# Top-32 attention and a PReLU block on one core: other MLP blocks, the last two pairs interleaved, other ticks for the preparation steps, two casts on another engine

## The chip, the cores and the metric

The kernel runs on one core of a Trainium2 chip. The metric is device microseconds (us) of that core. The kernel before took 1068.87, 1069.68 and 1070.53 us in three runs; the median is 1069.68 us. Five engines work side by side, each through its own list of instructions in order: TensorE (PE; its weight loads are PEld), VectorE (DVE), ScalarE (ACT), GpSimd (POOL) and SyncE (SP), which here only issues DMAs.

## The reference

Eight batches, eight heads, 576 rows of 64. Each row of scores keeps what reaches its 32nd largest value; the rest is masked. The result goes, as 4608 tokens of 512, through two matrix products with a PReLU between them.

```python
scores = scale * np.matmul(q, k.transpose(0, 1, 3, 2))
kth = np.partition(scores, -top_k, axis=-1)[..., -top_k:-top_k + 1]
scores = np.where(scores >= kth, scores, -1000000000.0)
attn = np.exp(scores - np.max(scores, axis=-1, keepdims=True))
attn = attn / (np.sum(attn, axis=-1, keepdims=True) + 1e-09)
x = np.matmul(attn, v)                      # (8, 8, 576, 64) -> (4608, 512)
h = x @ w_in
g = np.maximum(h, 0.0) + alpha * np.minimum(h, 0.0)
out = g @ w_out
```

## The kernel before

Two heads make a pair; 32 pairs of 9 tiles (128 rows by 576 columns; the ninth holds the last 64 rows of both heads) make 288 tiles. One loop turn, a tick n, emits for every engine a little work on different tiles, and each engine runs what it was given in the order of emission. So the order of the work is written out by hand:

- PE: the scores of tile n+1 (`scores`, L290 and L295, into one of two PSUM buffers), then what the calendar has for PE in this tick, then one step of the queue `back`.
- ACT: what the step of `back` in the tick before left for it, then three passes over the scores of tile n: Sign with a running sum (`act_a`, tile h, L303), the calendar's ACT steps, Exp (`act_e`, tile e, L313), and the scores plus a bias (`act_b`, tile b, L319), which needs the bias `be`.
- POOL: the bias `be` from the sum of h (L306), y = b*h of tile n-1 (`pool_y`, L328), then the calendar's POOL steps.
- DVE: the 8 largest of each of six segments of y of tile n-2 (L336), a merge of tile n-3 to the 24 largest (L351, L353), every third tick a choice of the threshold KP (`select`, L360 to L369), the masked weights w of tile n-6 (`weights`, L381, which reads b, KP and e), then the calendar's DVE steps, and last a tiny write into the next y buffer (`mark`, L323), after which POOL may fill that buffer.
- SP: loads of q, k and v (`load`, L132 to L140), DMA transposes of w (L386 to L391) and of the attention output (`x_turn`, L468 and L470), and the stores of the output (L563).

The calendar (`put` and `run`) holds the preparation of the coming pairs. `prep_plan` gives each step a tick by the table `ts`, counted from the pair's first tile: transposes of q and k (`pe_q`, `pe_k`, `pe_t` with their copies on ACT), casts of k and v to bf16 on POOL (`pool_k`, tile kb, L160; `pool_v`, tile v_bf, L163), a cast of q on POOL (`pool_q`, tile qTb, L198), statistics of the scores (`pe_g` to `dve_1`), the start threshold T0 (`pool_1`, `pool_1b` with a power of 9 values, L243, `pool_1c` with L247 and L248, and `dve_2`, L251), and two biases from it (`pool_2`).

The product of weights and v (`av`) and its normalisation on DVE (`av_out`) come 5 to 7 ticks after the fourth and the ninth tile of a pair. When the fourth pair of a batch is done, `x_turn` turns the batch's output, and the MLP blocks (`blocks`: seven of 512 tokens, then 448, 320, 256) whose tokens are there are put into `back`: 16 steps of four matmuls (`ph_step`) and three steps for each 128 tokens (`pz_step`). After tile 287 the loop goes on until `back` is empty. At the end a sum over all checks becomes a flag that every engine loads (L678 to L686); it decides whether a general path runs.

Of the kernel before, what the change touches and what calls it, by code (L numbers as in the profile page):

```python
# [27 lines left out]
def kernel(  # L28
# [24 lines left out]
    NX = 2560  # L53
# [41 lines left out]
    v_bfs = [prep.tile([128, 10, V1], BF16, name=f"v_bf{i}", bufs=1) for i in range(3)]  # L95
# [30 lines left out]
    def load(p):  # L126
# [15 lines left out]
        pairs[p] = dict(q=st_q, k=st_k, st_v=st_v, v=v_bfs[p % 3])  # L142

    def prep_plan(p):
# [137 lines left out]
    def scores(n):  # L282
        p, j = divmod(n, TPP)
# [25 lines left out]
    def act_e(n):  # L309
        p, j = divmod(n, TPP)  # L310
# [30 lines left out]
    def merge_ops(n):  # L341
        p, j = divmod(n, TPP)
# [28 lines left out]
    def weights(n):  # L371
        p, j = divmod(n, TPP)
# [23 lines left out]
    def check_pair(p, put_late):  # L396
# [6 lines left out]
        nc.vector.scalar_tensor_tensor(out=DD[:, kt, :, 0], in0=KP[:, ns], scalar=-1.0,  # L403
                                       in1=KP[:, ns], op0=ALU.mult, op1=ALU.max)
# [4 lines left out]
    def check_batch(b):  # L409
# [6 lines left out]
        for i, (jk, src, lim, op) in enumerate((  # L416
# [5 lines left out]
                                    accum_out=good[:, b, i:i + 1])  # L422

# [40 lines left out]
    def x_turn(b):  # L464
        for i in range(5):
# [66 lines left out]
    def mlp_steps(t0, tb):  # L532
        c0 = t0 % NX
        hold = {}

        def ph_step(f):
            if f == 0:
                hold["gT"] = mlp.tile([128, NFT, 512], BF16, name="gT", tag="gT", bufs=1)
            hold[f] = ph = mlp_bank("ph", tb)
            for kk in range(NKT):  # L540
                nc.tensor.matmul(ph, w_in_b[:, kk, f * 128:(f + 1) * 128], xT[:, kk, c0:c0 + tb],  # L541
                                 start=(kk == 0), stop=(kk == NKT - 1))

        def ph_act(f):
            nc.scalar.activation(hold["gT"][:, f, 0:tb], hold.pop(f), AF.Relu)  # L545
# [19 lines left out]
        for f in range(NFT):  # L565
# [7 lines left out]
    blocks = [(512 * i, 512) for i in range(7)] + [(3584, 448), (4032, 320), (4352, 256)]  # L573
# [5 lines left out]
    with tc.manual_schedule(engines={E.PE, E.Activation, E.DVE, E.Pool, E.SP}):  # L579
# [241 lines left out]
```

## Time and profile before

| | |
|---|---|
| median of three runs | 1069.68 us |
| profiled execution, its time | 1068.65 us |
| its span, first to last instruction | 1066.9 us |
| DVE busy | 926.2 us, 87% |
| PE busy | 840.2 us, 79% |
| ACT busy | 805.6 us, 76% |
| POOL busy | 711.9 us, 67% |
| mean granted TensorE clock | 0.918 |

Busy shares are means over a start, a long even stretch and an end in which DVE has nothing to do. Which engine bounds a stretch is seen from the one that has no idle time in it, and from who waits for whom there.

### The profile page before, as it was taken

The page shows a single profiled execution, that of the slowest core. Times are in us where ns is not written, and L with a number is a line of the kernel's source. Part 1 is how long each engine was busy: PE and PEld are TensorE (multiplying, and loading weights), DVE is VectorE, ACT ScalarE, POOL GpSimd, SP SyncE. Part 2 cuts the span into 40 slices and gives each one's busy share as a digit, 9 for nine tenths or more (in the row PEclk, how much of TensorE's full clock was granted, in tenths as well). Part 3 has the DMA queues.
Part 4 walks back from the last instruction along what each step waited for, and adds up shares of the span by engine and source line. Part 5 has one row for each costly group of instructions (what it writes and reads, how often), then busy time and mean ns, then how long its engine had stood idle before and what let it go on. Part 6 is the DMA issues. An engine that isn't in the chain of part 4 may idle for free.

```text
span 1066.9 us, 20165 instructions
## 1 busy us (share of the span) xinstructions
PE 840.2 (79%) x5188; PEld 486.5 (46%) x5255; DVE 926.2 (87%) x5228; ACT 805.6 (76%) x1611; POOL 711.9 (67%) x988
## 2 busy tenths in 40 slices
PE   4667787778877897788877896778877896778995
PEld 3344444445444454444544553445444554444453
DVE  3699979999999999999999999999999999999000
ACT  3998867788778878788778877888778877884332
POOL 3787757778767776787777776787777776773000
PEclk9867897899979998999889998999889997999998
DMA  5697433535464445544444455535453455224200
GB/s 130 123 174 149 100 76 79 110 75 83 105 104 82 87 109 104 96 84 90 108 88 86 85 114 101 98 80 106 97 95 74 93 104 110 51 56 102 68 27 28
DMA packets 343021, 99.48 MB, mean 93 GB/s; under 512 B 335201, under 2 KB 335217, under 8 KB 342897
## 3 DMA queue, kind: packets, MB, share of 16 engines
q1 hardware_dynamic: 341744, 96.01, 44.8%
q0 software_dynamic: 1152, 2.10, 1.3%
q8 instruction: 44, 0.72, 0.3%
q14 instruction: 81, 0.66, 0.2%
HBM read 36.71 MB, written 9.44 MB: 43 GB/s over the span
## 4 chain that ended last, share of the span: by engine, by line
DVE 65%; POOL 13%; PE 11%; issue 5%; ACT 4%; DMA 1%; SPq 0%; POOLq 0%; ACTq 0%
DVE C L336 16%; DVE w L381 14%; DVE L L351 8%; DVE C L353 7%; POOL y L328 5%; POOL sq L243 5%; PE pz L557 3%; PE ph L541 3%; DVE pr L365 3%; DVE kk L368 3%; PE ps L290 3%; DVE wm L381 2%; DVE P L210 2%; DVE EQ L360 2%; DVE T L251 2%
## 5 line engine op out<-in xcount | busy, mean ns | idle before, releaser
L328 POOL TENSOR_TENSOR y<-b,h 128x576 f32<-128x576 f32 x288 | 368.0, 1278 | 142.3 <-DVE y L323 135.5
L290 PE MATMUL ps<-qkT 128*128 128x288 f32 x1024 | 349.3, 469 | 126.9 <-ACT b L319 125.9
L336 DVE MAX8 C<-y 128x8 f32<-128x96 f32 x1728 | 423.4, 245 | 16.2 <-POOL y L328 16.2
L290 PEld LDWEIGHTS ps<-qkT 128*128 128x128 f32 x1024 | 199.0, 211 | 243.7 <-ACT b L319 201.0
L319 ACT ACTIVATE b<-ps,be 128x576 f32<-128x576 f32 x288 | 213.8, 742 | 120.3 <-POOL be L306 117.9
L381 DVE SCALAR_TENSOR_TENSOR w<-b,KP,e 128x576 bf16<-128x576 f32 x256 | 225.0, 879 | 0.0
L313 ACT ACTIVATE e<-ps,nbe 128x576 bf16<-128x576 f32 x288 | 215.4, 748 | 7.7 <-POOL nbe L258 3.0
L303 ACT ACTIVATE h<-ps,T 128x576 bf16<-128x576 f32 x288 | 213.5, 741 | 6.9 <-DVE T L251 6.1
L306 POOL TENSOR_SCALAR be<-S_all,n2t 128x1 f32<-128x1 f32 x288 | 144.8, 503 | 94.5 <-ACT h L303 93.2
L351 DVE MAX8 L<-C 128x8 f32<-128x48 f32 x864 | 164.4, 190 | 0.1
L541 PE MATMUL ph<-xT,w_in_b 128*128 128x512 bf16 (+3 forms) x606 | 150.9, 370 | 3.4 <-issue 1.5
L557 PE MATMUL pz<-w_out_b,gT 128*128 128x512 bf16 (+1 forms) x564 | 137.9, 379 | 2.2 <-issue 1.1
L545 ACT ACTIVATE gT<-ph 128x512 bf16<-128x512 f32 (+3 forms) x160 | 88.7, 555 | 30.6 <-PE ph L541 29.1
L353 DVE MATCH_REPLACE8 C<-L,C 128x48 f32<-128x48 f32 x576 | 109.7, 190 | 0.0
L541 PEld LDWEIGHTS <-w_in_b 128*128 128x128 bf16 x640 | 58.4, 100 | 53.5 <-issue 10.9
L557 PEld LDWEIGHTS <-gT 128*128 128x128 bf16 (+1 forms) x592 | 54.9, 98 | 60.5
L562 ACT COPY o_sb<-pz 128x512 f32<-128x512 f32 (+1 forms) x37 | 21.6, 582 | 65.0 <-PE pz L557 65.0
L303 ACT ACTIVATION_READ_ACCUMULATOR h<-ps,T 128x1 f32 x288 | 59.9, 208 | 0.0
L243 POOL TENSOR_TENSOR sq<-sq,half 128x9 f32<-128x9 f32 x32 | 58.5, 1829 | 0.2
L684 DVE TENSOR_SCALAR bad<-ptot 1x1 int32<-1x1 f32 x1 | 0.1, 145 | 65.8 <-PE ptot L683 65.8
L436 PEld LDWEIGHTS <-wT 128*128 128x128 bf16 x1280 | 51.6, 100 | 11.3 <-DMA wT<-w 3.1
L436 PE MATMUL pu<-v_bf,wT 128*128 128x65 bf16 x1280 | 53.7, 197 | 2.8 <-DMA wT<-w 2.8
(106 smaller groups left out, 981.1 us busy)
## 6 DMA issues: line engine op xcount, KB each, us to landing
out_dram<-o_sb SPq DMA_DIRECT2D x35, 256.0 KB, 2.3
st_q<-in_q_dram SPq DMA_DIRECT2D x64, 128.0 KB, 2.8
kst<-in_k_dram SPq DMA_DIRECT2D x64, 128.0 KB, 2.6
st_v<-in_v_dram SPq DMA_DIRECT2D x64, 128.0 KB, 2.5
w_stage<-in_moe_w_out_dram SPq DMA_DIRECT2D x16, 256.0 KB, 3.9
w_in_b<-in_moe_w_in_dram POOLq DMA_DIRECT2D x8, 256.0 KB, 6.0
wT<-w SPq DMA_TRANSPOSE x128, 3.3
st_q<-in_q_dram SPq DMA_DIRECT2D x32, 32.0 KB, 2.5
```

The lines of the kernel that those rows point to most:

```text
L290: nc.tensor.matmul(ps[:, hf, 0:HC], T[:, 0, c0:c0 + 128], T[:, 1 + j % 2, ks], start=True, stop=True)
L303: nc.scalar.activation(halves(t["h"]), t["ps"], AF.Sign, bias=T0[:, n:n + 1], scale=-ONE_EPS, accum_out=S_all[:, n:n + 1])
L306: nc.gpsimd.tensor_scalar(t["be"], S_all[:, n:n + 1], 512.5, d["n2t"][:, j:j + 1], ALU.is_le, ALU.mult)
L313: nc.scalar.activation(halves(t["e"]), t["ps"], AF.Exp, bias=d["nbe"][:, j:j + 1], scale=scl)
L319: nc.scalar.activation(halves(t["b"]), t["ps"], AF.Identity, bias=t["be"])
L328: nc.gpsimd.tensor_tensor(t["y"], t["b"], t["h"], ALU.mult)
L336: return [lambda g=g: nc.vector.max(out=C[:, j, g, :], in_=t["y"][:, g * SEG:(g + 1) * SEG]) for g in range(NSEG)]
L351: ops.append(lambda r=r, src=src: nc.vector.max(out=L[:, 8 * r:8 * r + 8], in_=src))
L353: ops.append(lambda r=r, src=src: nc.vector.match_replace(out=C2, in_to_replace=L[:, 8 * r:8 * r + 8], in_values=src, imm_value=NEG))
L381: nc.vector.scalar_tensor_tensor(out=dst, in0=t["b"], scalar=KP[:, n:n + 1], in1=t["e"], op0=ALU.is_ge, op1=ALU.mult)
L541: nc.tensor.matmul(ph, w_in_b[:, kk, f * 128:(f + 1) * 128], xT[:, kk, c0:c0 + tb], start=(kk == 0), stop=(kk == NKT - 1))
L557: nc.tensor.matmul(pz[0:m], hold["gT"][:, f, r0:r0 + m], w_out_b[:, f, :], start=False, stop=(f == NFT - 1))
```

## The change

- The MLP blocks follow the batches: for every two batches 512, 512 and 128 tokens, and for the last two 512, 320 and 320. A block of 128 tokens does four columns of w_in in a step. The ring buffer xT has 2304 columns (four batches) instead of 2560.
- The tiles of the last two pairs alternate (`ORDER`), so that the first four tiles of both come first. Their first half of the output is turned by its own, and the first block of 320 waits for that half only. Pair 31 is loaded and prepared some ten ticks earlier.
- In a tick the step of `back` is emitted before the calendar's PE steps, and two steps a tick after the last tile.
- The table `ts` is another; `av` comes one tick later (three ticks after the weights at the very end).
- The casts of k and v are `nc.scalar.copy` on ACT (`act_kb`, `act_v`), between h and e of a tick; v_bf has four buffers, y three, C three.
- The flag at the end is computed and loaded inside the loop (`final_flag`), some ticks before the last block ends.

```diff
-    NX = 2560
+    NX = 2304
...
+    ORDER = [divmod(n, TPP) for n in range(NT - 2 * TPP)]
+    ORDER += [(NPAIR - 2 + s, 2 * i + h) for i in range(4) for s in range(2) for h in range(2)]
+    ORDER += [(NPAIR - 2, 8), (NPAIR - 1, 8)]
...
-        def pool_k():
+        def act_kb():
             d["kb"] = prep.tile([128, 5, 130], BF16, name="kb", tag="kbP", bufs=1)
-            nc.gpsimd.tensor_copy(d["kb"], d["k"])
-
-        def pool_v():
-            nc.gpsimd.tensor_copy(d["v"][:, :, 0:D], d["st_v"])
+            nc.scalar.copy(d["kb"], d["k"])
+
+        def act_v():
+            nc.scalar.copy(d["v"][:, :, 0:D], d["st_v"])
...
-            ts = [-14, -13, -12, -11, -10, -9, -6, -5, -4, -3, -2, -2, -1, -5]
+            ts = [-14, -13, -12, -11, -10, -9, -7, -6, -5, -4, -3, -2, -1, -8,
+                  -13 if p == 3 else -15]
...
     def scores(n):
-        p, j = divmod(n, TPP)
+        p, j = ORDER[n]
...
-        y = attn.tile([128, S], FP32, name="y", bufs=4)
+        y = attn.tile([128, S], FP32, name="y", bufs=3)
...
+    def final_flag():
+        tot = const.tile([128, 1], FP32, name="tot")
+        junkg = const.tile([128, B * 4], FP32, name="junkg")
+        nc.vector.tensor_scalar(junkg, good.rearrange("p a b -> p (a b)"), 1.0, None, ALU.mult,
+                                ALU.add, accum_out=tot)
+        bad = const.tile([1, 1], I32, name="bad")
+        pt = ps_d.tile([1, 1], FP32, name="ptot", tag="pd")
+        nc.tensor.matmul(pt, tot, ones_f, start=True, stop=True)
+        nc.vector.tensor_scalar(bad, pt, float(128 * NT * (3 + NSEG)) - 0.5, None, ALU.is_lt)
+        flag.append(nc.values_load(bad[0:1, 0:1], min_val=0, max_val=1))
...
-    blocks = [(512 * i, 512) for i in range(7)] + [(3584, 448), (4032, 320), (4352, 256)]
+    blocks = []
+    for i in range(0, NTOK, 2 * S):
+        blocks += [(i, 512), (i + 512, 512), (i + 1024, 128)]
+    blocks[-2:] = [(NTOK - 640, 320), (NTOK - 320, 320)]
...
-            run(n, "pe")
-            if back:
-                pe_f, after = back.popleft()
-                pe_f()
+            for _ in range(2 if n >= NT else 1):
+                if back:
+                    if after:
+                        after()
+                    pe_f, after = back.popleft()
+                    pe_f()
+            run(n, "pe")
...
+                        dt = 3 if n >= NT - 7 else dt
                         put(n + dt, "pe", lambda wp=wp, g=g: av(wp, g))
                         put(n + dt + 1, "dve", lambda wp=wp, g=g: av_out(wp, g))
+                        if last and (g == 1 or wp == NPAIR - 1):
+                            part = (range(5) if wp < NPAIR - 1 else (range(2), range(2, 5))[g])
+                            put(n + dt + 1, "dve", lambda b=b, part=part: x_turn(b, part))
+                            lim = (b + 1) * S if g == 1 else NTOK - 320
...
+                            put(n + dt + (4 if wp < NPAIR - 1 else 2), "end", feed)
```

What the table moves is seen in the order of instructions on POOL, in four ticks in the middle of the program. Before, with v_bf and kb the casts, sq the statistics and DD a check; each `be` begins a tick:

```order
L163 CAST v_bf_110<-st_v_107 128x10x64
L306 TENSOR_SCALAR be<-S_all,n2t 128x1
L328 TENSOR_TENSOR y<-b,h 128x576
L238 TENSOR_TENSOR sq<-MM 128x9
L239 TENSOR_TENSOR sq<-MM,sq 128x9
L240 TENSOR_SCALAR sq<-sq 128x9
L160 CAST kb<-kst_104 128x650
L306 TENSOR_SCALAR be<-S_all,n2t 128x1
L328 TENSOR_TENSOR y<-b,h 128x576
L243 TENSOR_TENSOR sq<-sq,half 128x9
L405 TENSOR_TENSOR DD<-DD,C 128x9x6
```

and from the third tick on:

```order
L243 TENSOR_TENSOR sq<-sq,half 128x9
L405 TENSOR_TENSOR DD<-DD,C 128x9x6
L306 TENSOR_SCALAR be<-S_all,n2t 128x1
L328 TENSOR_TENSOR y<-b,h 128x576
L247 TENSOR_SCALAR sq<-sq 128x9
L248 TENSOR_TENSOR t_7962<-sq,MM 128x9
L198 CAST qTb<-qkT_111 128x576
```

After the change the same stretch of POOL reads:

```order
L242 TENSOR_TENSOR sq<-MM 128x9
L243 TENSOR_TENSOR sq<-MM,sq 128x9
L244 TENSOR_SCALAR sq<-sq 128x9
L312 TENSOR_SCALAR be<-S_all,n2t 128x1
L334 TENSOR_TENSOR y<-b,h 128x576
L247 TENSOR_TENSOR sq<-sq,half 128x9
L312 TENSOR_SCALAR be<-S_all,n2t 128x1
L334 TENSOR_TENSOR y<-b,h 128x576
L251 TENSOR_SCALAR sq<-sq 128x9
L252 TENSOR_TENSOR t_8003<-sq,MM 128x9
L418 TENSOR_TENSOR DD<-DD,C 128x9x6
```

The casts v_bf and kb are gone from POOL; the power (L243 before, L247 after) and the two steps behind it stand one tick earlier against the pair, and qTb alone is left behind y in the fourth tick.

The two casts stand on ACT, in the second and the fourth tick of a pair; there before, and now:

```order
L303 ACTIVATE h,S_all<-ps,T_100 128x576
L313 ACTIVATE e<-ps,nbe 128x576
L319 ACTIVATE b<-ps,be 128x576
L562 COPY o_sb<-pz 128x512
L303 ACTIVATE h,S_all<-ps,T_100 128x576
L313 ACTIVATE e<-ps,nbe 128x576
```

```order
L309 ACTIVATE h,S_all<-ps,T_100 128x576
L167 CAST v_bf_109<-st_v_107 128x10x64
L319 ACTIVATE e<-ps,nbe 128x576
L325 ACTIVATE b<-ps,be 128x576
L309 ACTIVATE h,S_all<-ps,T_100 128x576
L319 ACTIVATE e<-ps,nbe 128x576
L325 ACTIVATE b<-ps,be 128x576
L593 COPY o_sb<-pz 128x512
L309 ACTIVATE h,S_all<-ps,T_100 128x576
L164 CAST kb<-kst_104 128x650
L319 ACTIVATE e<-ps,nbe 128x576
L325 ACTIVATE b<-ps,be 128x576
```

A cast stands behind h, whose sum POOL's `be` needs, and ahead of e and b.

At the end of the program SP's queue shows where the last batch's output is turned (xT, from xb and xm) among the transposes of w and the stores of the MLP's output (o_sb). Before, and now:

```order
L563 DMA out_dram<-o_sb 128x512
L391 DMA_TRANSPOSE wT<-w_15294 128x9x128
L386 DMA_TRANSPOSE wTm<-wm 128x5x128
L387 DMA_TRANSPOSE wTm<-wm 128x4x128
L563 DMA out_dram<-o_sb 128x512
L468 DMA_TRANSPOSE xT<-xb 128x4x128 x4
L470 DMA_TRANSPOSE xT<-xm 128x4x64
L563 DMA out_dram<-o_sb 128x512 x3
```

```order
L494 DMA_TRANSPOSE xT<-xb 128x4x128 x2
L594 DMA out_dram<-o_sb 128x512 x2
L397 DMA_TRANSPOSE wT<-w_15518 128x9x128
L594 DMA out_dram<-o_sb 128x512
L397 DMA_TRANSPOSE wT<-w_15578 128x9x128
L594 DMA out_dram<-o_sb 128x512
L392 DMA_TRANSPOSE wTm<-wm 128x5x128
L393 DMA_TRANSPOSE wTm<-wm 128x4x128
L392 DMA_TRANSPOSE wTm<-wm 128x5x128
L393 DMA_TRANSPOSE wTm<-wm 128x4x128
L494 DMA_TRANSPOSE xT<-xb 128x4x128 x2
L496 DMA_TRANSPOSE xT<-xm 128x4x64
```

Two of the five transposes now stand ahead of the last transposes of w, and the transposes of the last ninth tiles stand behind the stores of the block that runs at that time.

## Rows read from the trace of the kernel before

**Rows 1.** The page's 40 slices of the span, DVE's busy tenths:

```profile
DVE  3699979999999999999999999999999999999000
```

**Rows 2.** Busy us (xcount) of PE, PEld, DVE, ACT, POOL; then PEclk, DMA:

```profile
163.00:281.00 118.00, 94.80 (x590) 55.35 (x599) 114.32 (x642) 95.42 (x191) 88.18 (x120) 0.90 0.48 93
```

**Rows 3.** Who waited for whom, 163 to 940 us: total, times, longest:

```profile
ACT b L319 <- POOL be L306: 103.9, 155, 3.0
```

**Rows 4.** Groups of DVE, 163 to 940 us: busy, mean ns, idle before:

```profile
L381 DVE SCALAR_TENSOR_TENSOR w<-b,KP,e 128x576 bf16<-128x576 f32 x209 | 183.8, 879 | 0.0
...
L369 DVE TENSOR_TENSOR KP<-kk 128x3 f32<-128x3 f32 x79 | 22.8, 289 | 2.7
...
L251 DVE TENSOR_SCALAR T<-t 128x9 int32<-128x9 int32 x26 | 15.6, 601 | 11.5 <-POOL t L248 11.5
```

**Rows 5.** Timeline of DVE and POOL: start, us, engine, line, operation, idle before:

```profile
600.37 0.16 DVE L369 TENSOR_TENSOR KP<-kk 128x3 f32<-128x3 f32 x1
...
602.84 0.80 DVE L381 SCALAR_TENSOR_TENSOR w<-b,KP,e 128x576 bf16<-128x576 f32 x1
...
605.98 0.72 POOL L163 CAST v_bf<-st_v 128x640 bf16<-128x640 f32 x1
...
606.16 1.14 DVE L381 SCALAR_TENSOR_TENSOR w<-b,KP,e 128x576 bf16<-128x576 f32 x1
...
609.78 0.73 POOL L160 CAST kb<-kst 128x650 bf16<-128x650 f32 x1
...
609.97 0.55 DVE L369 TENSOR_TENSOR KP<-kk 128x3 f32<-128x3 f32 x1
...
615.27 1.28 POOL L328 TENSOR_TENSOR y<-b,h 128x576 f32<-128x576 f32 x1
...
616.07 1.08 DVE L381 SCALAR_TENSOR_TENSOR w<-b,KP,e 128x576 bf16<-128x576 f32 x1
...
617.51 0.66 POOL L198 CAST qTb<-qkT 128x576 bf16<-128x576 f32 x1
617.60 0.60 DVE L251 TENSOR_SCALAR T<-t 128x9 int32<-128x9 int32 x1 [0.45 <-POOL t L248]
...
943.24 0.17 DVE L251 TENSOR_SCALAR T<-t 128x9 int32<-128x9 int32 x1 [0.44 <-POOL t L248]
```

**Rows 6.** Groups of ACT, 163 to 940 us, columns as in Rows 4:

```profile
L319 ACT ACTIVATE b<-ps,be 128x576 f32<-128x576 f32 x236 | 175.1, 742 | 106.0 <-POOL be L306 103.9
...
L562 ACT COPY o_sb<-pz 128x512 f32<-128x512 f32 x24 | 14.0, 582 | 18.2 <-PE pz L557 18.2
```

**Rows 7.** Timeline of the start, columns as in Rows 5:

```profile
5.13 0.58 ACT L156 COPY qkT<-pq 128x512 f32<-128x512 f32 x1 [3.11 <-PE pq L153]
...
6.68 0.72 POOL L160 CAST kb<-kst 128x650 bf16<-128x650 f32 x1 [3.76 <-DMA kst<-in_k_dram]
...
23.82 0.28 PE L479 MATMUL aps<-ident_f,a 16*128 16x16 f32 x1 [6.31 <-DMA a<-in_moe_alpha_dram]
```

**Rows 8.** Timeline of the end, PE, ACT and DVE, columns as in Rows 5:

```profile
965.42 1.04 PE L553 MATMUL pz<-w_id_b,xT 128*128 128x512 bf16 x4
...
971.26 0.80 PE L436 MATMUL pu<-v_bf,wT 128*128 128x65 bf16 x20
...
999.11 3.62 PE L557 MATMUL pz<-w_out_b,gT 128*128 128x512 bf16 x16
...
1015.72 10.08 PE L541 MATMUL ph<-xT,w_in_b 128*128 128x320 bf16 x64
...
1038.81 0.61 PE L541 MATMUL ph<-xT,w_in_b 128*128 128x256 bf16 x4
...
1052.68 3.62 PE L557 MATMUL pz<-w_out_b,gT 128*128 128x512 bf16 x16
...
1056.38 0.58 ACT L562 COPY o_sb<-pz 128x512 f32<-128x512 f32 x1 [3.73 <-PE pz L557]
...
1057.24 0.14 DVE L684 TENSOR_SCALAR bad<-ptot 1x1 int32<-1x1 f32 x1 [65.83 <-PE ptot L683]
```

More of the change, by code (lines that the diff above doesn't have):

```diff
@@ L94 @@
     st_vs = [prep.tile([128, 10, D], FP32, name=f"st_v{i}", bufs=1) for i in range(2)]
-    v_bfs = [prep.tile([128, 10, V1], BF16, name=f"v_bf{i}", bufs=1) for i in range(3)]
+    v_bfs = [prep.tile([128, 10, V1], BF16, name=f"v_bf{i}", bufs=1) for i in range(4)]
     qkTs = [prep.tile([128, 3, S], FP32, name=f"qkT{i}", bufs=1) for i in range(3)]
@@ L309, in act_e @@
     def act_e(n):
-        p, j = divmod(n, TPP)
+        p, j = ORDER[n]
         t, d = tiles[n], pairs[p]
@@ L330, in seg_ops @@
     def seg_ops(n):
-        p, j = divmod(n, TPP)
+        p, j = ORDER[n]
         if j == 0:
-            pairs[p]["C"] = prep.tile([128, TPP, NSEG, 8], FP32, name="C")
+            pairs[p]["C"] = prep.tile([128, TPP, NSEG, 8], FP32, name="C", bufs=3)
         C = pairs[p]["C"]
@@ L402, in check_pair @@
         DD = DDs[b]
-        nc.vector.scalar_tensor_tensor(out=DD[:, kt, :, 0], in0=KP[:, ns], scalar=-1.0,
-                                       in1=KP[:, ns], op0=ALU.mult, op1=ALU.max)
+        n0, sd = NT - 2 * TPP, p - NPAIR + 2
+        parts = [(DD[:, kt, :, 0], KP[:, ns])]
+        if sd >= 0:
+            parts = [(DD[:, kt, 0:8, 0].rearrange("p (a c) -> p a c", a=4),
+                      KP[:, n0:n0 + 16].rearrange("p (a c) -> p a c", a=4)[:, :, 2 * sd:2 * sd + 2]),
+                     (DD[:, kt, 8:9, 0], KP[:, n0 + 16 + sd:n0 + 17 + sd])]
+        for o_, k_ in parts:
+            nc.vector.scalar_tensor_tensor(out=o_, in0=k_, scalar=-1.0, in1=k_,
+                                           op0=ALU.mult, op1=ALU.max)
         put_late(lambda: nc.gpsimd.tensor_tensor(
@@ L462, in av_out, with x_turn @@
                 rz[0:64, 4:6].unsqueeze(2).to_broadcast([64, 2, D]), ALU.mult)
-    def x_turn(b):
-        for i in range(5):
+    def x_turn(b, chunks):
+        for i in chunks:
             c0 = (b * S + 128 * i) % NX
@@ L533, in mlp_steps @@
         c0 = t0 % NX
+        fpp = 512 // tb if tb <= 256 else 1
         hold = {}
@@ L563, in pz_act @@
             nc.sync.dma_start(out[t0 + r0:t0 + r0 + m, :], o_sb[0:m])
-        for f in range(NFT):
+        for f in range(0, NFT, fpp):
             yield (lambda f=f: ph_step(f)), (lambda f=f: ph_act(f))
@@ L610 @@
             p, j = divmod(n, TPP)
-            if j == 0 and p + 2 < NPAIR:
-                load(p + 2)
-                plan(p + 2)
+            if j == 0 and p + 2 < NPAIR - 1 or n == NT - 34:
+                nxt = NPAIR - 1 if n == NT - 34 else p + 2
+                load(nxt)
+                plan(nxt)
             tail[0] = n >= NT
@@ L674 @@
     main.close()
-    tot = const.tile([128, 1], FP32, name="tot")
-    junkg = const.tile([128, B * 4], FP32, name="junkg")
-    nc.vector.tensor_scalar(junkg, good.rearrange("p a b -> p (a b)"), 1.0, None, ALU.mult,
-                            ALU.add, accum_out=tot)
-    bad = const.tile([1, 1], I32, name="bad")
-    with tc.tile_pool(name="ps_f", bufs=1, space=PS) as ps_f:
-        pt = ps_f.tile([1, 1], FP32, name="ptot")
-        nc.tensor.matmul(pt, tot, ones_f, start=True, stop=True)
-        nc.vector.tensor_scalar(bad, pt, float(128 * NT * (3 + NSEG)) - 0.5, None, ALU.is_lt)
-    flag = nc.values_load(bad[0:1, 0:1], min_val=0, max_val=1)
-    with tc.If(flag > 0):
+    with tc.If(flag[0] > 0):
         with tc.For_i(0, B, 1) as bi:
```

67 lines of the change are left out of this document (36 added, 31 removed).

## The prediction

> **What bounds the kernel now.** I read the slices first. DVE is at nine tenths or more from the second slice to the 37th and at zero in the last three [rows 1], so there are two kernels in one: an even stretch that DVE sets, and an end of some 80 us in which it does nothing. The busy times of one piece of the even stretch agree: of 118 us DVE works 114.3, ACT 95.4, PE 94.8, POOL 88.2 [rows 2]. The waits show ACT waiting for POOL's bias, 103.9 us in all between 163 and 940 us [rows 3]; that is slack of ACT, since POOL itself is held back by DVE's marks. So in the even stretch only what shortens DVE's own line counts, and that line holds more than its work, which the groups of DVE and then single rows of one pair show. T waits 11.5 us for POOL in 26 pairs. Three groups have means far above their short instances: w 879 ns where a clean one takes 0.80 us, KP 289 ns against 0.16, T 601 ns against 0.17 [rows 4, 5]. The excess is 183.8 - 209 x 0.80 = 16.6 us for w, 22.8 - 79 x 0.16 = 10.2 for KP, 15.6 - 26 x 0.17 = 11.2 for T. With T's wait that is 49.5 us, 1.9 us a pair.
>
> The single rows say where the excess comes from. The w of 1.14 us begins 0.18 us into POOL's cast of v (605.98, 0.72 us); the KP of 0.55 begins 0.19 into the cast of k; the T of 0.60 begins 0.09 into the cast of q; the w of 1.08 begins 0.8 into a late y and outlasts it by 0.6 [rows 5]. Each of these DVE instructions stands still until POOL's pass over some 600 columns is nearly done.
>
> The Trainium skill, page "SBUF — State Buffer", section "Who interferes with whom", has a rule for this: a VectorE instruction with two SBUF inputs and a GpSimd instruction that reads SBUF take the same port in turn, the first one keeps it for its whole length, and ScalarE waits for nobody. The long w agrees, by 0.34 us. T has one input, and is held too.
>
> **The change part by part: the even stretch.** The trace has 26 pairs in it between 163 and 940 us (T x26, [rows 4]).
> - The cast of k leaves POOL: KP's 10.2 us go.
> - The cast of v leaves POOL: of the two long w in a pair, the one at 1.14 goes, 0.34 x 26 = 8.8 us.
> - T's input comes a tick earlier (the power and the two steps behind it move, T stays): its wait of 11.5 us goes.
> - The cast of q stays, but stands straight behind y instead of behind L248, where the cast of v stood in its tick, and so meets w instead of T: 11.2 us go, 8.8 come, 2.4 are won.
> - The second long w (1.08 - 0.80 = 0.28, 7.3 us in all) comes from a y that is late because POOL does the power of 9 values in a short tick. The power now stands in a tick in which DVE has the choice of KP and two small instructions besides; I count half, 3.6 us.
>
> Sum 36.5 us, 1.4 us a pair. From below, only T's wait is certain to go (11.5); from above, all of 49.5. I stay nearer the upper end, because the long rows stand beside those two casts in every pair, not here and there.
>
> What this costs is on ACT: no row shows a cast of 650 columns from SBUF there. The nearest are the copy of 512 columns, 582 ns, and the pass of 576 columns with a bias, 742 ns [rows 6]; bounds 0.58 and 0.84 (0.742 x 650/576), and I take 0.70, 1.4 us a pair. The cover is ACT's idle time, 118 - 95.4 = 22.6 us in four pairs (777 us / 26 = 29.9 us each), 5.6 us a pair, of which 4.0 (103.9/26) are the wait for the bias [rows 2, 3]. With 1.4 more work and a pair 1.4 us shorter, 2.8 us of it are left, so I count nothing. Behind a cast queue e and b of its tick; y of that tile waits for b, and the next scores wait for the PSUM buffer that b frees.
>
> The Trainium skill's page "ScalarE: Activation LUTs", section "What ACT_TABLE_LOAD costs", gives an estimate of 0.186 us + 0.833 ns a column, less an overlap of 0.09 us: 0.63 us a cast, 1.3 us a pair; the sum would not change.
>
> Ahead of 163 us, where the weights are prepared, ACT has more to do and DVE idles for other reasons; the pairs there may win up to 5 us, and I take 1.5. In the last 30 us of the stretch two pairs are prepared at the same time, and PE takes the product with v three ticks after the weights instead of five or six; I add 1 us, between 0 and 4.
>
> Reversing PE's order in a tick (MLP step, then calendar), y with three buffers and the ring of 2304 columns cost nothing: the transposes are needed a tick later, the mark stands where it stood, and a block still reads only columns that are four batches from the next write.
>
> **The start.** The cast of k of pair 0 is now ACT's first instruction. POOL could begin it at 6.68 us, when k had landed, while ACT copied q from 5.13 on [rows 7]. The copy of q comes after the cast, at about 7.4, and with it all that leads to the first threshold: 2.3 us. The cast of v stands ahead of the first h as well and needs DVE's late memsets; SP's third load of v waits for it, and behind that load the alpha vector, for which PE stood until 23.82 [rows 7]. That chain moves by about as much, so I take 2.5 us in all; bounds 1 (the first ticks have slack) and 5 (both casts add up).
>
> **The end.** PE does nothing but MLP from 965.42, when the last scores are out, until 1056.3, when the copy of the last block can begin: 90.9 us [rows 8]. In the changed order PE has behind its last scores: 13 and then 60 matmuls of 512 columns for the rest of the 512 block, at 3.62/16 = 0.22 us, 16.1 us; two blocks of 320, each 1038.81 - 1015.72 = 23.1 us, 46.2; 80 small matmuls of three products with v, at 0.80/20 = 0.04, 3.2 us [rows 8]. The flag in the middle makes PE and ACT wait for a value that goes PE, DVE, load: at least the 0.3 us from the last copy's end to `bad`, at most the 9.5 us from `bad` to the end of the span; nearer the first, 1.5. In SP's queue the transposes of the last ninth tiles stand behind the stores of the 512 block, whose last store is ready some 17.5 us after the last scores (16.1, 0.8 for one product with v and 0.6 for the copy); four transposes behind it make the two products with v about 2 us late. Sum 69.0 us instead of 90.9: 21.9 us won, with 16 and 25 as ends. The turned first half is there in time, since 16 us of the older block cover it. Since the flag is loaded early, the last copy is followed by the branch at once: 1 us won, between 0 and 2.
>
> **The sum.** The profiled execution took 1068.65 us with a span of 1066.9. 1068.65 - 36.5 - 1.5 + 1.0 + 2.5 - 21.9 - 1.0 = 1011.3; the median of the runs lies 1.0 above the profiled execution, so 1012 us.
>
> **The rivals.**
> - The collisions only move. In the ticks of the casts e and b are 0.7 us later, y of that tile begins later, and w meets y there as it does at 616.07 [rows 5]. For it: w starts so soon after y that any delay of y counts. Against: at the row of 615.27 y was late because of POOL, not of ACT. It takes back 10.2 + 8.8 = 19.0 us: 1031 us.
> - ACT becomes the bound at today's pace: a pair takes what it takes now, and only the end is won. For it: ACT's ticks are uneven, and a tick with a cast and an MLP pass is longer than DVE's short ticks. Against: 5.6 us of idle time a pair. 1012 + 38 = 1050 us.
> - The end is held by DVE and SP: the products with v wait for transposes, PE stands in order behind them, and of 21.9 us only 8 are won. Against: 73 matmuls of the older block and 28 of the next stand ahead of the first product that can wait. 1026 us.
> - Slower: the casts stand on the path, because b is what frees the PSUM buffer of the scores; then both casts lengthen each pair by up to 1.4 us, 26 x 1.4 = 36 us, on top of the second rival: 1086 us. It decides from (1069.7 - 1050)/26 = 0.76 us a pair on. Against it: ACT's wait for the bias stands right where the cast is put and shrinks by the same time.
>
> **How the numbers follow.** Forecast 0.65; collisions move 0.17; end held 0.07; ACT at today's pace 0.07; slower 0.04. The forecast's own range, from the bounds of the stretch (25 to 46 us), of the end and of the start, is 999 to 1027. The range reaches over the first rival, 998 to 1035, and leaves out the second, the fourth and the edges of the forecast. A difference of 0.2%, 2 us, is about what a measurement of this kernel can tell from none. Only the passage from the second rival to the fourth lies near 1070: 0.01 for no difference, 0.04 for slower, 0.95 for faster.
>
> **What would show it.** The means of DVE's groups: KP near 160 ns, T near 170 ns with no idle time ahead of it, w near 840 ns with one long instance in a pair, beside the cast of q. A pair of 28 us. Two cast groups on ACT near 0.7 us, and ACT's wait for the bias well below 100 us. Some 69 us from PE's last scores to the last copy, with one wait for the flag. The first h about 4 us later, the alpha transpose 2 to 3 us later. It is wrong if C waits for y in the middle of the program (ACT or POOL is then the bound), or if w stays near 880 ns.

## The result and the profile after

The changed kernel took 1008.03 to 1009.91 us in four runs, median 1009.41; the kernel before, on the same chip, 1070.01. The ratio is 0.943 (95% interval 0.9417 to 0.9449): faster by 60.6 us, where 1012 was predicted. The profiled execution took 1008.03 us, its span is 1006.3.

Where the time went is read by cutting both spans at the same events. POOL's power of 9 values runs once in a pair and is an easy mark; "power p" is the start of that of pair p.

| stretch | before, us | after, us | difference | predicted |
|---|---|---|---|---|
| start to power 1 | 47.0 | 49.3 | +2.3 | +2.5 |
| power 1 to power 5 | 121.4 | 114.9 | -6.5 | -1.5 |
| power 5 to power 29 (24 pairs) | 710.8 | 677.5 | -33.3 | -33.7 |
| power 29 to the end of the last scores | 86.3 | 88.5 | +2.2 | -1.8 |
| last scores to the last matmul | 90.8 | 69.7 | -21.1 | -21.9 |
| last matmul, its copy, end of span | 10.6 | 6.4 | -4.2 | -1.0 |

(In the last column the third row is 36.5 x 24/26 = 33.7; the fourth is the other two pairs' 2.8 off and the 1.0 that the prediction adds.) The even stretch and the end carry the gain. How far the rows repeat is seen in the kernels below whose edits leave a stretch alone: three of them have 677.3 or 677.4 us from power 5 to power 29. From power 1 to power 5 the kernel that has only its flag at another place, at the end, takes 116.2 us instead of 114.9, and the clock granted to TensorE there is a mean of 0.75 of full speed instead of 0.81; so one or two us in that row are not told from none.

Of the 40 slices of DVE, which answer to [rows 1], only the last two are without work instead of the last three:

```profile
DVE  3598989999999999999999999999999999999800
```

The window of [rows 2], read again (columns PE, PEld, DVE, ACT, POOL, clock, DMA):

```profile
163.00:281.00 118.00, 96.73 (x631) 58.49 (x641) 115.97 (x677) 104.02 (x209) 86.04 (x117) 0.93 0.48 94
```

DVE is still the one without idle time, and gets through 677 instructions in it instead of 642. ACT went from 95.4 to 104.0 us. Over the whole even stretch, 163 to 905 us here, its wait for the bias shrank from 103.9 us [rows 3] to 70.1, while POOL's wait for DVE's marks shows who sets the pace:

```profile
POOL y L334 <- DVE y L329: 174.5, 187, 2.0
ACT b L325 <- POOL be L312: 70.1, 88, 3.3
```

The groups of DVE that answer to [rows 4], between 163 and 905 us, and the casts on ACT:

```profile
L387 DVE SCALAR_TENSOR_TENSOR w<-b,KP,e 128x576 bf16<-128x576 f32 x208 | 170.4, 819 | 0.0
...
L255 DVE TENSOR_SCALAR T<-t 128x9 int32<-128x9 int32 x27 | 16.0, 592 | 2.0 <-POOL t L252 2.0
L375 DVE TENSOR_TENSOR KP<-kk 128x3 f32<-128x3 f32 x79 | 12.8, 162 | 2.7
```

```profile
L325 ACT ACTIVATE b<-ps,be 128x576 f32<-128x576 f32 x236 | 175.8, 745 | 72.2 <-POOL be L312 70.1
...
L167 ACT CAST v_bf<-st_v 128x640 bf16<-128x640 f32 x26 | 19.3, 741 | 0.0
L164 ACT CAST kb<-kst 128x650 bf16<-128x650 f32 x25 | 18.5, 740 | 0.0
```

w is nearly clean (819 ns against 879), KP is clean (162 against 289), T no longer waits but is as long as it was. Why T is still long is seen in four rows of the timeline:

```profile
621.25 1.28 POOL L334 TENSOR_TENSOR y<-b,h 128x576 f32<-128x576 f32 x1
...
622.21 0.93 DVE L387 SCALAR_TENSOR_TENSOR w<-b,KP,e 128x576 bf16<-128x576 f32 x1
622.48 1.19 POOL L202 CAST qTb<-qkT 128x576 bf16<-128x576 f32 x1
623.06 0.63 DVE L255 TENSOR_SCALAR T<-t 128x9 int32<-128x9 int32 x1
```

w begins in the last third of y and loses 0.13 us. The cast of q begins 0.27 us after w, and now the cast stands still: it takes 1.19 us instead of 0.66 [rows 5]. It ends at 623.67, and T, queued behind w, ends just behind it, at 623.69.

The start, against [rows 7]:

```profile
6.33 1.28 ACT L164 ACT_TABLE_LOAD   x1 [6.33 <-DMA kst<-in_k_dram]
7.62 0.73 ACT L164 CAST kb<-kst 128x650 bf16<-128x650 f32 x1
8.26 0.58 ACT L160 COPY qkT<-pq 128x512 f32<-128x512 f32 x1
...
21.67 0.74 ACT L309 ACTIVATE h<-ps,T 128x576 bf16<-128x576 f32 x1
...
25.99 0.28 PE L505 MATMUL aps<-ident_f,a 16*128 16x16 f32 x1 [6.27 <-DMA a<-in_moe_alpha_dram]
```

The first row is ACT's table load, which ran at 0.74 us in the kernel before. The copy of q is 3.1 us later (8.26 against 5.13), the alpha transpose 2.2, the first h 5.1 (21.67 against 16.58).

The end, against [rows 8]:

```profile
929.01 1.19 PE L301 MATMUL ps<-qkT 128*64 128x288 f32 x8 [0.22 <-ACT b L325]
...
953.95 0.72 PE L467 MATMUL pu<-v_bf,wTm 128*64 128x65 bf16 x10 [2.19 <-DMA wTm<-wm]
...
963.06 0.70 PE L570 MATMUL ph<-xT,w_in_b 128*128 128x320 bf16 x4 [0.88 <-DVE bad L447]
...
996.29 3.62 PE L588 MATMUL pz<-w_out_b,gT 128*64 128x512 bf16 x16
```

PE has two waits of note behind its last scores: 2.19 us for the transposes of the last ninth tile, 0.88 for the flag. From the last scores to the last matmul it works 66.1 us instead of 86.1, so nearly all of the gain there is work that is no longer left over.

### The profile page after: what moved, and what is told of

It is laid out like the page before. It is cut to its first block, busy times and chain, and to the rows that moved or that the text cites. A ratio compares the mean times of both kernels' runs of the same rounds, so it can differ in the third digit from the quotient of the medians.

```text
span 1006.3 us, 20180 instructions
## 1 busy us (share of the span) xinstructions
PE 816.2 (81%) x5315; PEld 488.2 (49%) x5383; DVE 898.3 (89%) x5235; ACT 834.3 (83%) x1671; POOL 657.1 (65%) x924
## 4 chain that ended last, share of the span: by engine, by line
DVE 81%; PE 7%; issue 4%; POOL 3%; ACT 2%; DMA 1%; SPq 1%; ACTq 0%; POOLq 0%
DVE C L342 21%; DVE w L387 18%; DVE L L357 11%; DVE C L359 10%; DVE pr L371 3%; DVE kk L374 3%; DVE xb L479 2%; DVE wm L387 2%; PE pz L588 2%; DVE P L214 2%; DVE EQ L366 2%; PE ph L570 2%; DVE T L255 2%; PE pl L536 1%; DVE KP L375 1%
## 5 line engine op out<-in xcount | busy, mean ns | idle before, releaser
L296 PE MATMUL ps<-qkT 128*128 128x288 f32 x1024 | 341.7, 460 | 138.1 <-ACT b L325 134.9
L296 PEld LDWEIGHTS ps<-qkT 128*128 128x128 f32 x1024 | 187.8, 204 | 229.8 <-ACT b L325 195.4
L319 ACT ACTIVATE e<-ps,nbe 128x576 bf16<-128x576 f32 x288 | 217.9, 756 | 8.6 <-POOL nbe L262 5.2
L309 ACT ACTIVATE h<-ps,T 128x576 bf16<-128x576 f32 x288 | 216.1, 750 | 1.3 <-PE ps L296 1.2
L387 DVE SCALAR_TENSOR_TENSOR w<-b,KP,e 128x576 bf16<-128x576 f32 x256 | 209.7, 819 | 0.0
L570 PE MATMUL ph<-xT,w_in_b 128*128 128x512 bf16 (+2 forms) x734 | 147.7, 326 | 2.9 <-DVE bad L447 0.9
L312 POOL TENSOR_SCALAR be<-S_all,n2t 128x1 f32<-128x1 f32 x288 | 101.1, 351 | 47.5 <-ACT h L309 44.0
L576 ACT ACTIVATE gT<-ph 128x512 bf16<-128x512 f32 (+1 forms) x156 | 88.8, 569 | 14.3 <-PE ph L570 11.8
L570 PEld LDWEIGHTS <-w_in_b 128*128 128x128 bf16 x768 | 67.6, 98 | 61.6 <-issue 7.5
L247 POOL TENSOR_TENSOR sq<-sq,half 128x9 f32<-128x9 f32 x32 | 59.0, 1844 | 0.3
L462 PEld LDWEIGHTS <-wT 128*128 128x128 bf16 x1280 | 50.9, 102 | 11.4 <-issue 2.2
L301 PE MATMUL ps<-qkT 128*64 128x288 f32 x256 | 42.1, 454 | 5.7 <-ACT b L325 5.5
```

Source lines behind the costliest of these rows:

```text
L296: nc.tensor.matmul(ps[:, hf, 0:HC], T[:, 0, c0:c0 + 128], T[:, 1 + j % 2, ks], start=True, stop=True)
L319: nc.scalar.activation(halves(t["e"]), t["ps"], AF.Exp, bias=d["nbe"][:, j:j + 1], scale=scl)
L387: nc.vector.scalar_tensor_tensor(out=dst, in0=t["b"], scalar=KP[:, n:n + 1], in1=t["e"], op0=ALU.is_ge, op1=ALU.mult)
L462: nc.tensor.matmul(pu[:, 2 * i + side, :], wT[:, 4 * side + c, :], v_bf[:, 5 * side + c, :], start=(c == 0), stop=(c == 4))
L570: nc.tensor.matmul(hold[f][:, i, :], w_in_b[:, kk, (f + i) * 128:(f + i + 1) * 128], xT[:, kk, c0:c0 + tb], start=(kk == 0), stop=(kk == N ...
```

## Experiments

The theory: in the even stretch some of DVE's instructions (w, KP and T so far) stand still when they begin while POOL passes over SBUF, until that pass is nearly done, so the time follows from which instruction meets which pass; ACT has room for the casts. Not every DVE instruction is held: from 164 to 842 us the changed kernel's MAX8 on y take 0.23 to 0.26 us, all 1298 of them, most beside a y that POOL is making. Rivals: that POOL's amount of work or its lateness is what counts; that ACT is at its bound. Pair times below are power 5 to power 29, divided by 24: 29.62 us before, 28.23 after. "After" is the changed kernel.

**Casts back on POOL, at their old ticks.**

```diff
-            nc.scalar.copy(d["kb"], d["k"])
+            nc.gpsimd.tensor_copy(d["kb"], d["k"])
...
-            nc.scalar.copy(d["v"][:, :, 0:D], d["st_v"])
+            nc.gpsimd.tensor_copy(d["v"][:, :, 0:D], d["st_v"])
...
-            ts = [-14, -13, -12, -11, -10, -9, -7, -6, -5, -4, -3, -2, -1, -8,
-                  -13 if p == 3 else -15]
+            ts = [-14, -13, -12, -11, -10, -9, -7, -6, -5, -4, -3, -2, -1, -5,
+                  -13]
```

> The changed kernel with the casts of k and v back on POOL, at the ticks where they stood before. Theory (DVE is held by POOL's passes): the long KP (0.55) and the long w (1.14) come back, 0.39 + 0.34 = 0.73 us a pair, some 28 pairs: +20 us, less about 2 us that the start gains; 1024 to 1030 us, KP's mean near 290 ns. Rival (the other ticks of T made the gain, the place of the casts is worth nothing): within 3 us of 1009.

(In this kernel pair 29 multiplies with the v of pair 31, whose load now stands ahead of the cast; the work in a pair is the same.) Measured 1023.55 us (ratio 0.957, 0.9554 to 0.9583), 14 us more than after and just under the range; a pair of 28.85. The size came nearly as expected, the place did not: KP stayed at 162 ns and w at 0.82. With the statistics a tick earlier, the cast of k comes behind the power, and another instruction meets it, once in a pair (DD, a check; 0.17 us in the changed kernel):

```profile
831.14 0.76 POOL L164 CAST kb<-kst 128x650 bf16<-128x650 f32 x1
831.23 0.70 DVE L416 SCALAR_TENSOR_TENSOR DD<-KP 128x9 f32<-128x9 f32 x1
```

In 24 pairs DD takes 12.3 us more of DVE's line, of the 15.0 that the stretch lost.

**Statistics at their old ticks, casts on ACT.**

```diff
-            ts = [-14, -13, -12, -11, -10, -9, -7, -6, -5, -4, -3, -2, -1, -8,
+            ts = [-14, -13, -12, -11, -10, -9, -6, -5, -4, -3, -2, -2, -1, -8,
```

> The changed kernel with the statistics of a pair (from the second product to T's input) at their old ticks, one later than now; the casts stay on ACT. Theory (two separate causes, waits and held instructions): T's wait of 0.44 us and a y made late by the power come back, 0.15 to 0.3: +0.5 to 0.7 us a pair, 14 to 20 us, 1023 to 1029 us. Rival (with the casts gone POOL is quick enough at the old ticks): within 4 us of 1009, T without idle time ahead of it.

Measured 1046.82 us (0.979, 0.9771 to 0.9801): 37 us lost, twice what was expected; a pair of 29.50. T's wait came back (10.6 us in 24 pairs), but most of the loss is a w that was not expected, once in each pair (18.5 us):

```profile
852.01 1.83 POOL L247 TENSOR_TENSOR sq<-sq,half 128x9 f32<-128x9 f32 x1
...
854.38 1.28 POOL L334 TENSOR_TENSOR y<-b,h 128x576 f32<-128x576 f32 x1
...
854.63 1.64 DVE L387 SCALAR_TENSOR_TENSOR w<-b,KP,e 128x576 bf16<-128x576 f32 x1
```

The power, 1.83 us for 9 values, makes the next y late; y then begins 0.25 us ahead of w and holds it for almost its whole length. In this kernel the product with v stays a tick later, as in the changed one, so the tick of the power has 0.55 us less work on DVE, and w comes 0.25 us behind the start of y instead of 0.80 [rows 5]. That w, 1.64 us instead of 1.08, hides most of what the casts win in this kernel. Taken back from the changed kernel one at a time, the ticks cost 1.27 us a pair and the casts 0.62; against before, the kernel with the new ticks alone wins 0.77, the one with the casts alone 0.12, the one with both 1.39. The two are not independent, and the 0.12 is not what the casts would win if the product with v had kept its tick; no run shows that.

**An extra pass on POOL.** In 28 pairs POOL does one more pass of 640 columns, into a buffer that nobody reads, straight behind y: a cast of v in one kernel, a memset in the other.

```diff
+    scr = prep.tile([128, 10, D], BF16, name="scr", bufs=1)
...
+        def pool_x():
+            nc.gpsimd.tensor_copy(scr, d["st_v"])    # or: nc.gpsimd.memset(scr, 0.0)
...
+        if 3 <= p < NPAIR - 1:
+            ts.append(-8)
+            steps.append(dict(pool=[pool_x]))
```

> POOL gets one more cast of 640 columns a pair (28 pairs, of v, into a buffer that nobody reads), straight behind y in a tick where w stands on DVE, while the casts on ACT stay. Theory (a POOL pass over SBUF holds a DVE instruction that begins behind it until it ends): one long w of 1.14 us more a pair, +0.34 x 28 = 9.5 us, 1019 us (1014 to 1024), although POOL has idle time. Rival (it was POOL's work or its lateness that cost, not the overlap): 1008 to 1012 us, and w's mean stays near 0.82 us.

> The same as the extra cast, at the same place, but the POOL instruction is a memset of 640 bf16 columns, which writes SBUF and reads nothing. By the rule that only a POOL instruction that reads SBUF holds a DVE instruction with two SBUF inputs: no long w at it, 1008 to 1012 us. By the rival that any POOL pass over SBUF holds DVE: as with the cast, 1014 to 1024 us. If it is much shorter than 0.7 us, the hold is scaled by its length.

The cast: 1016.75 us (0.950, 0.9486 to 0.9517), 7.3 more than after, in the theory's range; a pair of 28.51. The memset: 1008.13 us (0.943, 0.9416 to 0.9448), no difference, a pair of 28.23. Both passes begin 0.2 us ahead of a w, and are of like length:

```profile
638.37 0.72 POOL L168 CAST scr<-st_v 128x640 bf16<-128x640 f32 x1
638.59 1.10 DVE L394 SCALAR_TENSOR_TENSOR w<-b,KP,e 128x576 bf16<-128x576 f32 x1
```

```profile
631.77 0.63 POOL L168 MEMSET scr<- 128x640 bf16 x1
632.01 0.82 DVE L394 SCALAR_TENSOR_TENSOR w<-b,KP,e 128x576 bf16<-128x576 f32 x1
```

POOL's work and lateness do not count by themselves; a pass that reads SBUF does. The Trainium skill, page "SBUF — State Buffer", section "Who interferes with whom", says just this: a VectorE instruction with two SBUF inputs contends with a GpSimd instruction that reads SBUF, and not with one that only writes it. The two runs agree.

**The cast of q on ACT too.**

```diff
-            nc.gpsimd.tensor_copy(d["qTb"], d["qkT"][:, 0, :])
+            nc.scalar.copy(d["qTb"], d["qkT"][:, 0, :])
...
-                 dict(act=[act_t], pe=[pe_g], pool=[pool_q]), dict(act=[act_g], pe=[pe_r]),
+                 dict(act=[act_t, pool_q], pe=[pe_g]), dict(act=[act_g], pe=[pe_r]),
```

> The third cast, of q (qTb), goes from POOL to ACT as well, behind the copy of T's input. Theory (what is left of the holds hangs on qTb): T falls from 0.59 to 0.17 us, the w beside it from 0.93 to 0.80, 0.55 us a pair, 28 pairs: 12 to 15 us less, 994 to 998 us. Rival (with the third cast ACT becomes the bound, or the hold moves to another DVE instruction): 1005 us or above, with T at 0.17 all the same.

Measured 999.15 us (0.934, 0.9325 to 0.9362), 10.3 less than after and just above the theory's range; a pair of 27.80. T is clean in all pairs; w beside it is not, since it was never the cast that it met, but the end of y:

```profile
615.60 1.27 POOL L334 TENSOR_TENSOR y<-b,h 128x576 f32<-128x576 f32 x1
616.54 0.95 DVE L387 SCALAR_TENSOR_TENSOR w<-b,KP,e 128x576 bf16<-128x576 f32 x1
...
617.41 0.16 DVE L255 TENSOR_SCALAR T<-t 128x9 int32<-128x9 int32 x1
```

T's 0.47 us in 24 pairs make 11.2; w lost 0.8, and the stretch won 10.2.

**T one more tick earlier.**

```diff
-            ts = [-14, -13, -12, -11, -10, -9, -7, -6, -5, -4, -3, -2, -1, -8,
+            ts = [-14, -13, -12, -11, -10, -9, -8, -7, -6, -5, -4, -3, -2, -8,
```

> The steps from the power of 9 values to T0 are one more tick earlier; qTb then starts right behind y and ahead of w instead of beside T. Theory (a DVE instruction is held by the POOL pass that it begins behind): T falls to 0.17 us, a gain of 0.42 a pair, but the w beside qTb is held from its beginning, and takes 1.1 instead of 0.93; net 0.2 us a pair, some 1003 us, between 997 and 1009. Rival (qTb's hold of T was covered, since DVE waits for y in the next tick): no difference, or slower.

Measured 1013.94 us (0.947, 0.9452 to 0.9489): slower by 4.5 than after, which neither theory gave for the reason that is seen. T is clean (168 ns), and the cast of q meets neither w nor T. But there is a new chain in most pairs: y holds a w, that w holds the power, which takes 2.34 us instead of 1.83, and the late y behind the power holds EQ, the first instruction of the choice of KP (0.29 us elsewhere):

```profile
619.69 1.28 POOL L334 TENSOR_TENSOR y<-b,h 128x576 f32<-128x576 f32 x1
...
620.47 1.11 DVE L387 SCALAR_TENSOR_TENSOR w<-b,KP,e 128x576 bf16<-128x576 f32 x1
...
620.93 2.34 POOL L247 TENSOR_TENSOR sq<-sq,half 128x9 f32<-128x9 f32 x1
...
623.53 1.27 POOL L334 TENSOR_TENSOR y<-b,h 128x576 f32<-128x576 f32 x1
...
624.11 0.85 DVE L366 TENSOR_TENSOR EQ<-S_all,iota 128x144 bf16<-128x144 f32 x1
```

In 24 pairs T gives back 11.2 us, EQ costs 10.6 and w 2.6, so the even stretch is 2.3 us longer. Another part, 3.8 us, was lost between power 1 and power 5, where the granted clock was 0.77 instead of 0.81; that part was not traced.

**Each cast on ACT twice.**

```diff
             nc.scalar.copy(d["kb"], d["k"])
+            nc.scalar.copy(d["kb"], d["k"])
...
             nc.scalar.copy(d["v"][:, :, 0:D], d["st_v"])
+            nc.scalar.copy(d["v"][:, :, 0:D], d["st_v"])
```

> Every cast of k and v on ACT is done twice, one behind the other: 1.5 us more work on ACT a pair, in the two ticks that hold a cast. Theory (in the even stretch ACT has idle time that covers the casts): ACT is left with some 3 us of idle time a pair, so the time stays between 1009 and 1016 us; the wait of b for POOL's bias (70 us) shrinks again. Rival (the casts have already brought ACT to its bound, or stand on the path through b and the PSUM buffer): each pair is longer by 1.3 to 1.5 us, 27 pairs, some 1044 to 1050 us.

Measured 1017.47 us (0.951, 0.9481 to 0.9528), somewhat above the range. In the even stretch nothing was lost, a pair took 28.27 us, and ACT's idle time paid for it: from 170 to 850 us its wait for the bias is 28.0 us, where it was 62.0 in the changed kernel:

```profile
ACT b L327 <- POOL be L314: 28.0, 56, 2.4
```

The loss lies ahead of it: 2.0 us up to power 1, 6.5 from there to power 5. There ACT also prepares the MLP's weights. From power 1 to power 5 it works 109.1 us instead of 102.2, and its idle time is 12.3 us against 12.7, so the second casts were added to the time there. Idle time that it has is no cover: most of it is spent in its order, waiting for PE's products of the weights, 8.0 us in the changed kernel and 9.7 here:

```profile
ACT w_id_b L542 <- PE pl L538: 9.7, 4, 3.3
```

So ACT has room for a second pair of casts from pair 5 on, and not before. A part of the 6.5 us may be the granted clock, 0.76 in this stretch against 0.81.

**The end.** One kernel without the alternation of the last two pairs (the first half is still turned by its own, but later), one with the flag computed behind the last block.

```diff
-    ORDER = [divmod(n, TPP) for n in range(NT - 2 * TPP)]
-    ORDER += [(NPAIR - 2 + s, 2 * i + h) for i in range(4) for s in range(2) for h in range(2)]
-    ORDER += [(NPAIR - 2, 8), (NPAIR - 1, 8)]
+    ORDER = [divmod(n, TPP) for n in range(NT)]
```

> The changed kernel with the tiles of the last two pairs one pair after the other; the MLP blocks, the early preparation of the last pair and the split turn stay. Theory (the alternation lets the first block of 320 begin without a wait): the turned half comes some 20 us after the last scores instead of 12, PE has 16 us of older work, so it waits 4 to 8 us: 1013 to 1017 us. Rival (the smaller backlog of MLP work alone made the end shorter): within 2 us of 1009.

```diff
-                        if b == B - 1:
-                            put(n + 6, "end", final_flag)
...
+        final_flag()
```

> The changed kernel with the flag computed and loaded after the last block, as before. Theory (the engines fetch the code behind the branch while PE still works, when the flag is there early): from the last store's copy to the end 9.9 us again instead of 5.7, less the 1.1 us that ACT and PE wait for the flag in the middle: +3 us, 1012 to 1013 us. Rival (the early flag saves only the load of the value, 1 us, and costs as much in the middle): 1009 to 1010 us.

Without the alternation 1013.12 us (0.948, 0.9462 to 0.9488), 3.7 more than after: its last matmul ends 75.3 us after the last scores instead of 69.7. The first half's transposes are issued 20.9 us after the last scores instead of 10.4, and the first block of 320 waits for them:

```profile
955.44 5.92 PE L568 MATMUL ph<-xT,w_in_b 128*128 128x320 bf16 x24 [7.32 <-DMA xT<-xb]
```

PE's work behind the last scores is 66.8 us, as good as the 66.1 of the changed kernel. So the theory's wait is there, and of the 21.1 us won at the end the alternation keeps 5.6; the others come from the smaller rest of work (86.1 us before), which the rival had alone.

With the flag at the end 1009.63 us (0.944, 0.9427 to 0.9453): no difference, as the rival had it. The time from the end of the last copy to the end of the span is 6.9 us there, 5.7 after and 9.9 before: the early flag saves 1.2 at the end, and PE pays 0.88 for it on the way. The other 3 us are not the flag's place. A part is that the sum no longer waits for the last copy: `bad` was at 1057.24 before, behind the copy's end at 1057.0 [rows 8], and in this kernel stands ahead of it:

```profile
1000.69 0.15 DVE L447 TENSOR_SCALAR bad<-ptot 1x1 int32<-1x1 f32 x1 [39.81 <-PE ptot L446]
```

From `bad` to the end it is 7.4 us here and 9.7 before; that difference stays open.

**The start.** The casts of pair 0 alone back on POOL.

```diff
+        if p == 0:
+            steps[13:] = [dict(pool=[pool_v]), dict(pool=[pool_k])]
```

> Pair 0's casts of k and v go back to POOL, as in the kernel before; all other pairs keep them on ACT. Theory (the copies of q behind the cast of k, and the alpha load behind the cast of v, delay the start by 2.3 us): the first h comes 4 to 5 us earlier than at 21.7, the whole takes 2 to 2.5 us less, some 1007 us. Rival (the first ticks have slack, and DVE idles there for other reasons): within 1 us of 1009.4.

Measured 1005.27 us (0.941, 0.9396 to 0.9432), 4.1 less than after, more than the 2 to 2.5 expected; the profile has 3.0 of them up to power 1. The copy of q and the first h are back where they stood before the change, and the table load ran at 0.73 us:

```profile
5.25 0.58 ACT L160 COPY qkT<-pq 128x512 f32<-128x512 f32 x1 [3.23 <-PE pq L157]
...
16.79 0.74 ACT L318 ACTIVATE h<-ps,T 128x576 bf16<-128x576 f32 x1 [6.06 <-DVE T L262]
```

**Together.** The last three edits that touch preparation in one kernel (pair 0's casts on POOL, q's cast on ACT, T one tick earlier), and then the two that had gained, q's cast on ACT from pair 4 on.

> Three edits at once: pair 0's casts on POOL, T one tick earlier, and the cast of q on ACT, which took 10 us off alone. Theory (the gains add up where they lie in different places: start -2, q -10, T's tick -2 to -4): 991 to 996 us. Rival (with q's cast on ACT nothing is left that T's tick could win, or ACT, which now has three casts in neighbouring ticks, makes b late): 997 to 1002 us.

> The two edits that gained alone, without the one that lost: pair 0's casts of k and v on POOL (4.1 us less alone), and the casts of q on ACT from pair 4 on (10.3 us less alone; in the first four pairs, where ACT has the weights to prepare, q stays on POOL, which cost about 1 us between the power of pair 1 and that of pair 5 when it went). Theory (the start and the even stretch lie one behind the other, so the gains add): 1009.4 - 4.1 - 10.3 - 1.0 = 994, between 992 and 997 us, a pair of 27.8 us from pair 5 on. Rival (the gain at the start is given back when ACT's copies of q become the limit): 998 to 1000 us. T moved one tick earlier is left out: it lost 4.5 us alone.

The three together took 1013.74 us (0.948, 0.9464 to 0.949), outside both ranges and 16.8 us more than the kernel with two of them (which keeps q's cast on POOL in the first four pairs). Most of that is T's tick, which cost only 4.5 alone: EQ behind the late y takes 13.9 us in 24 pairs here and took 10.6 there, but the 11.2 us at T that paid for it are already won by q's cast. The two took 996.91 us (0.933, 0.9313 to 0.9351), the fastest here, 12.5 below after and 73 below before. A pair takes 27.83 us, as with q's cast alone. Of the 4.1 us of the start only 2.2 are left, and the interval holds both theories: power 1 comes 3.0 us earlier than in the kernel with q's cast alone, power 5 only 0.4. In between ACT's waits are longer (9.1 us for the weights' products against 7.4, 1.4 for a load against 0.3), but this is the stretch in which one or two us are not told from none, so where the gain went stays open.

## Why the prediction was right

The time came out 2.6 us under the forecast. The mechanism and the large terms were right; that the whole is so near is in part luck, since wrong terms cancel, in the stretch and between the rows.

- **Which engine bounds, and by what.** Right, and shown: DVE bounds, a POOL pass that reads SBUF holds it, and only overlap counts (extra cast against extra memset).
- **KP, 10.2 us.** Measured 12.8 - 79 x 0.16 = 0.2 us of excess left; 10.0 gone.
- **w, 3.6 net (8.8 off, 8.8 on, 3.6 for the late y).** Mis-sized: the excess fell from 16.6 to 170.4 - 208 x 0.80 = 4.0 us, so 12.6 gone. The power in its new tick makes hardly any y late; the step "I count half" should have been nearly all, and the cast of q put nothing on w: with that cast gone the same w still takes 0.95 us.
- **T, 11.2 off.** Wrong. "And so meets w instead of T": it meets w, but w was first, so the cast stood still, outlasted w and held T as before (16.0 - 27 x 0.17 = 11.4 us). The prediction had the rule that the first one keeps the port, and used it in one direction only. The trace of before shows the other direction: the step of POOL that begins while the long w runs takes 0.77 us, and 0.28 in the changed kernel, where it begins ahead of w:

```profile
616.52 0.77 POOL L247 TENSOR_SCALAR sq<-sq 128x9 f32<-128x9 f32 x1
```

```profile
619.60 0.28 POOL L251 TENSOR_SCALAR sq<-sq 128x9 f32<-128x9 f32 x1
```

These two errors, +9 and -11, nearly cancel, which is luck.

- **T's wait, 11.5.** 9.5 gone.
- **Sum of the stretch.** 10.0 + 12.6 - 0.2 + 9.5 = 31.9 us by these groups, 36.5 predicted, 1.39 us a pair measured against 1.40. Cut at power 5 and power 29, and with each DVE instruction counted from the end of the one before it to its own end, the account closes: w 11.7, KP 9.2, T's wait 10.6, T 1.2 (it now begins before w has ended) and wm, the w of the ninth tile, 0.5, together 33.2 of the 33.3 us.
- **ACT's cost, nothing.** Right in the even stretch: a cast takes 0.74 us instead of 0.70, and even a second one costs nothing. Wrong as a statement on the kernel: pair 0's casts cost 4.1 us, and ahead of pair 5 a second cast is not covered. The first one is, in pairs 1 to 4: with the casts on POOL the stretch from power 1 to power 5 was 119.1 us, not shorter than 114.9.
- **Ahead of 163 us, -1.5.** It won 6.5. The bound of 5 was too low; the experiment with the statistics at their old ticks has 123.5 us from power 1 to power 5 instead of 114.9, the one with the casts on POOL 119.1, so this too hangs on both, and more on the ticks.
- **The start, +2.5.** Measured +2.3 up to power 1. What was not seen is that the table load stands behind the first cast's wait: the copy of q came 3.1 us later instead of 2.3, the first h 5.1 instead of 4.
- **From power 29 to the last scores, -1.8.** Measured +2.2. The sum added 1.0 for two pairs prepared at once and counted on 2.8 from the last two of its 26 pairs; where the 4 us went was not traced.
- **The end, -21.9.** Measured -21.1. The 2 us for late transposes are 2.19, the flag 0.88 where 1.5 was taken. Without the alternation it would be 5.6 us worse.
- **The flag's branch, -1.0.** The end behind the last copy is 4.2 us shorter, more than the bound of 2; 1.2 belong to the early flag, and 2.3 stay open.
- **Rivals.** The collisions of the two casts did not move in the changed kernel; that collisions can was shown twice, in other kernels (DD beside the cast of k, EQ beside the late y). ACT at the old pace, the end held, and slower: all fell.

## What to carry to other kernels

Where one engine has no idle time, list its instructions that are longer than their shortest instance, find the pass of the neighbour that each overlaps, and price a change by which instruction meets which pass afterwards, in both directions: the one that starts first makes the other stand, and what is queued behind the loser is late as well. The rows here give the price: in each of the fifteen collisions in the rows shown, the held instruction ends as if it had begun 0.12 to 0.20 us ahead of the end of the one that holds it (for the w of 1.64 us: y ends at 855.66, and w at 856.27, which is 0.80 after 855.47). Moving a small slow step by a tick can be worth more than moving a whole pass to another engine (taken back one at a time here, 1.27 us a pair against 0.62), because it decides whether the next pass is late. A pass moved to an engine with room in the even stretch may stand on the path in the start; leave it where it was there.

## What was not expected of the hardware

- The hold works both ways and reaches one instruction further: POOL's cast of 576 columns takes 1.19 us instead of 0.66 when it begins 0.27 us behind a w of 0.93.
- POOL's memset of 640 columns, 0.63 us, does not lengthen a w that begins 0.24 us behind it (0.82 us); a cast of the same shape, 0.72 us, does (1.10).
- POOL's power on 9 values a partition takes 1.83 us, reads SBUF, and holds no DVE instruction itself; it costs through the y behind it. So the rule as the prediction gives it, that the first one keeps the port for its whole length, does not cover it. In the kernel before:

```profile
612.90 1.83 POOL L243 TENSOR_TENSOR sq<-sq,half 128x9 f32<-128x9 f32 x1
...
613.14 0.80 DVE L381 SCALAR_TENSOR_TENSOR w<-b,KP,e 128x576 bf16<-128x576 f32 x1
```

- ACT's table load (1.28 us) stood behind the wait of the activation that it precedes: it ran at 6.33 us, when k had landed, and so on the path; where the copy of q comes first it ran at 0.74.
